# Windowed attention and a SoLU layer on one core: the second and fourth tile's first product in two other PSUM banks, the opening's list laid out anew, the last eviction by ScalarE alone

## The chip, the cores and the metric

The kernel runs on one core of a Trainium2 chip. The metric is the device time of one execution in microseconds. The engines are TensorE (PE; its weight loads are shown as PEld), VectorE (DVE), ScalarE (ACT), GpSimd (POOL) and SyncE (SP, which here only issues DMAs). Each engine works through its own instructions in order and waits on semaphores for the others. PSUM, into which TensorE writes, has eight banks of 512 float32 per partition.

## The reference

Two parts, one after the other. First, attention with a causal window over 8 batches, 8 heads, 576 positions and 64 channels per head; heads 0 to 3 look back over 32 neighbouring positions, heads 4 to 7 over 32 positions that lie 4 apart:

```python
scores = scale * np.matmul(q, k.transpose(0, 1, 3, 2))
rel = pos[:, None] - pos[None, :]
mask_plain = (rel >= 0) & (rel < window)                                  # window = 32
mask_dil = (rel >= 0) & (rel < window * dilation) & (rel % dilation == 0) # dilation = 4
scores = np.where(masks[None, :, :, :], scores, -1000000000.0)
scores = scores - np.max(scores, axis=-1, keepdims=True)
attn = np.exp(scores)
attn = attn / (np.sum(attn, axis=-1, keepdims=True) + 1e-09)
return np.matmul(attn, v)
```

Its result, 4608 tokens of 512 values (8 heads of 64), is the input x of the second part:

```python
h = x @ w_in                                   # 512 -> 1024
e = np.exp(h - h_max)
sm = e / (np.sum(e, axis=-1, keepdims=True) + 1e-09)
solu = h * sm
mu = np.mean(solu, axis=-1, keepdims=True)
var = np.mean((solu - mu) ** 2, axis=-1, keepdims=True)
ln = (solu - mu) / np.sqrt(var + 1e-06) * g_ln
return (ln @ w_out)                            # 1024 -> 512
```

The weights w_in and w_out arrive as 64-bit floats, and the kernel turns them into 32-bit ones on the chip.

## The kernel before, in words

**Attention in units.** A unit is a pair of heads of one batch; there are 32 (`n` = 0 to 31), four to a batch, of which the first two are plain and the last two dilated. For each unit the steps are: `S` (scores, TensorE, lines 175 to 198, into banks 2 and 3), `mask` (DVE), `max` (DVE), `sub` (subtract the maximum), `exp` (ACT), `sum` and `inv` (DVE), `norm` (multiply by the inverse sum), `turn` (32x32 transposes, DVE), `V` (the product with v, TensorE, line 265, into banks 4 to 7), `xh` (ACT, the rounded high part of the result, line 283) and `xl` (DVE, what the rounding left over, line 286). For units 0 to 3 TensorE itself adds the mask (line 183), so `mask` is empty and `sub` runs on DVE; for the others `mask` is a DVE instruction and `sub` runs on Pool. `norm` runs on DVE, unless a unit is in `POOL_NORM`, which is empty.

**The second part in tiles.** A tile is 128 tokens; there are 36 (`i` = 0 to 35). The first product (lines 293 to 305) has 24 matmuls, in four groups of six: `ha`, `hb` make the left half of the 1024 columns (bank 0), `hc`, `hd` the right half (bank 1). `ha` and `hc` read the part of x that comes from units 0 and 1 of the batch, `hb` and `hd` that from units 2 and 3. Each product is made of three, high by high, high by low and low by high, so that the result is nearly that of full float32. Then `peak` (DVE, the row maximum, line 310), `e` (ACT, exponential, line 317), `gate` (DVE, the product of both, line 324, which is the last to read banks 0 and 1), `mid` (centring, on ACT for tiles 0 to 3, otherwise on DVE), `var` (ACT, with six small instructions on Pool), `t` (eight transposes on TensorE into banks 3 and 4, line 357), `th` (ACT) and `tl` (DVE), which copy the high and the low part of the transposed tile, `o` (the second product, 24 matmuls, line 387, bank 2) and `out` (ACT scales, SP stores). `ps_h` is one pair of banks, 0 and 1, for all tiles, so the first product of a tile can begin only when the gate of the tile before has been read.

**The weights.** Each of 16 blocks (`b`; 0 to 7 of w_in, of which b//2 is the group of 128 input channels and b%2 the column half; 8 to 15 of w_out) is loaded (`w`, 512 KB) and converted: `low` and `abs` (ACT), `sign`, `clamp`, `join` (DVE), for w_out also `gain` (ACT), then `hi` (ACT, the rounded high part) and the low part. The latter goes one of two ways, by `LOW_DIFF`: for "m" TensorE makes the difference in PSUM with an identity (`diff`, lines 475 and 476, bank 5 + b % 3) and ACT copies it (`lo`, line 482); for "p" Pool subtracts (`lo`, line 484). So `hd0`, the last group of the first tile's first product, needs blocks 0 to 7 and units 0 to 3. The words of block b lie in a buffer that is shared: blocks 6 to 11 take those of blocks 0 to 5, blocks 12 and 13 those of 8 and 9, blocks 14 and 15 those of 10 and 11, and a load waits until its buffer has been read.

**The order.** It is written out by hand: `INIT` (first loads) and `OPENING` (everything up to the second product of tile 4) are lists of words, a step and its number, and the instructions of each engine are issued in the order of these words (lines 517 to 519). A word such as `S4` is one unit's scores; `q8`, `v8`, `w6` are loads, all of which stand in SP's one queue; a load of q, k or v takes the buffer of the unit four before and waits until that has been read. From tile 6 on (`FIRST`) the fixed list `STEP` is gone through once for each tile; tile 35 and what follows have `LAST` and `END`. When the opening's list ends, units 0 to 9 have been through `turn`, units 0 to 8 through `xl`, the second product has been made for tiles 0 to 4, and tile 5 has been transposed. The next words are `ha6` and the rest of the step for tile 6.

**The end.** The last tile's result lies in bank 5 and is evicted by `moe_out_last` in two halves, one by ACT and one by DVE, and stored in two halves, one on ACT's queue and one on SP's.

Of the kernel before, what the change touches and what calls it, by code (L numbers as in the profile page):

```python
# [14 lines left out]
AF = mybir.ActivationFunctionType  # L15
ALU = mybir.AluOpType
# [10 lines left out]
NTILE = NTOK // P  # L27
# [10 lines left out]
PE_MASK = (0, 1, 2, 3)  # L38
POOL_SUB = True
POOL_NORM = ()  # L40
# [42 lines left out]
def windowed_attention_then_solu_kernel(  # L83
# [13 lines left out]
    nc = tc.nc  # L97
# [16 lines left out]
    mask_sb = const.tile([P, 2, NS * WQ], BF16, name="mask_sb")  # L114
# [9 lines left out]
    ps_h = banks[:, 0:2, :]  # L124
# [471 lines left out]
```

## Time and profile before

| | us |
|---|---|
| median of three runs | 567.88 (567.01 to 571.52) |
| the profiled execution | 567.52 |
| its span, from the first to the last instruction | 565.7 |
| TensorE busy, share of the span | 531.3, 94% |
| VectorE busy | 358.2, 63% |
| ScalarE busy | 237.3, 42% |
| GpSimd busy | 110.6, 20% |
| mean granted TensorE clock | 0.982 |

A row of a group names line, engine, operation, output <- inputs by the program's names, shapes and count, then the busy time, the mean of one in ns, the idle time of the engine ahead of it and what ended most of that. A row of the timeline gives start and length in us, and in brackets the idle time of the engine before it and its releaser. A row of the chain gives start, length and the work. A row of the waits says which instruction waited for which: us in total, times, the longest. A row of the windows gives the busy time of each engine in a stretch of the span, then the granted clock, the share of the DMA engines and GB/s. Durations include some overlap: the next instruction of an engine starts before the one before has ended by the profile.

### The profile page before, as it was taken

How to read it: one execution, taken by the hardware profiler on the slowest of the kernel's cores; microseconds unless marked ns; L12 is line 12 of the kernel's file. 1: busy time of each engine (PE TensorE's matmuls, PEld its weight loads, DVE VectorE, ACT ScalarE, POOL GpSimd, SP SyncE). 2: the span in 40 equal slices, each digit the busy share in tenths (PEclk: the TensorE clock that was granted, in tenths of full speed). 3: DMA queues.
4: the chain of work that ended last, by engine and by line, in shares of the span. 5: the costliest groups of instructions: out<-in, count | busy, mean ns of one | idle time of the engine just before them, and what ended most of it. 6: DMA issues, size and time to landing. Idle time of an engine off the chain costs nothing.

```text
span 565.7 us, 16593 instructions
## 1 busy us (share of the span) xinstructions
PE 531.3 (94%) x7424; PEld 422.9 (75%) x7424; DVE 358.2 (63%) x555; ACT 237.3 (42%) x386; POOL 110.6 (20%) x256
## 2 busy tenths in 40 slices
PE   2775799899999999999999999999999999999997
PEld 1443588678888888888888888888888888888885
DVE  2989865576667766567667766567667766533342
ACT  3679754334344333433344333433344333433232
POOL 0002451123112222112112222112112222111111
PEclk9799889899999999999999999999999999999999
DMA  8976102332322233112222222123321000001001
GB/s 304 399 287 237 57 1 93 110 103 93 93 93 92 93 93 93 48 64 93 92 93 93 93 92 93 48 65 93 93 93 48 21 21 21 20 19 38 19 20 37
DMA packets 22103, 51.66 MB, mean 91 GB/s; under 512 B 2704, under 2 KB 3216, under 8 KB 22032
## 3 DMA queue, kind: packets, MB, share of 16 engines
q1 hardware_dynamic: 21888, 50.48, 26.4%
q8 instruction: 58, 0.95, 0.7%
q10 hardware_dynamic: 144, 0.13, 0.1%
q14 instruction: 13, 0.11, 0.1%
HBM read 41.16 MB, written 9.44 MB: 89 GB/s over the span
## 4 chain that ended last, share of the span: by engine, by line
PE 88%; DVE 5%; ACT 3%; issue 2%; DMA 1%; SPq 1%; ACTq 0%
PE banks L299 36%; PE banks L387 36%; PE banks L357 5%; PE banks L265 5%; PE banks L191 5%; DMA id_sb<-ident 1%; DVE x_lo L286 1%; DVE low L450 1%; DVE mag L458 1%; ACT x_hi L283 1%; PE banks L475 1%; DVE mag L443 1%; ACT low L437 0%; ACT w_i L482 0%; DVE nmax L310 0%
## 5 line engine op out<-in xcount | busy, mean ns | idle before, releaser
L299 PE MATMUL banks<-w_i,x_hi 128*128 128x512 f32 x576 | 188.9, 409 | 8.3 <-DVE mu L324 7.7
L387 PE MATMUL banks<-w_o,th 128*128 128x512 f32 x576 | 183.0, 401 | 0.0
L299 PEld LDWEIGHTS banks<-w_i,x_hi 128*128 128x128 f32 x576 | 105.1, 192 | 31.6 <-DVE mu L324 8.1
L387 PEld LDWEIGHTS banks<-w_o,th 128*128 128x128 f32 x576 | 107.0, 189 | 23.9
L299 PE MATMUL banks<-w_i,x_lo 128*128 128x512 f32 x288 | 115.0, 399 | 0.6 <-DVE x_lo L286 0.5
L387 PE MATMUL banks<-w_o,tl 128*128 128x512 f32 x288 | 112.8, 395 | 0.0
L310 DVE TENSOR_REDUCE nmax<-banks 128x1 f32<-128x1024 f32 x36 | 44.1, 1224 | 66.9 <-PE banks L299 66.9
L230 ACT ACTIVATE sm<-sm 128x640 f32<-128x640 f32 x32 | 23.5, 737 | 132.0 <-POOL sm L226 128.6
L317 ACT ACTIVATE e<-banks,nmax 128x1024 f32<-128x1024 f32 x36 | 40.2, 1117 | 65.9 <-DVE nmax L310 62.9
L372 DVE TENSOR_TENSOR tl<-banks,th 128x512 fp32r<-128x512 f32 x72 | 46.4, 685 | 32.3 <-ACT th L364 32.3
L299 PEld LDWEIGHTS banks<-w_i,x_lo 128*128 128x128 f32 x288 | 55.1, 191 | 14.3 <-DVE x_lo L286 1.4
L226 POOL TENSOR_TENSOR sm<-sm,mx 128x640 f32<-128x640 f32 x28 | 35.4, 1263 | 151.0 <-DVE mx L217 150.9
L387 PEld LDWEIGHTS banks<-w_o,tl 128*128 128x128 f32 x288 | 54.5, 189 | 12.8
L341 ACT ACTIVATE e<-t 128x1024 f32<-128x1024 f32 x36 | 38.2, 1061 | 49.6 <-DVE t L336 49.5
L205 DVE TENSOR_TENSOR sm<-banks,mask_sb 128x640 f32<-128x640 f32 x28 | 23.1, 824 | 54.5 <-PE banks L191 54.4
L364 ACT CAST th<-banks 128x512 fp32r<-128x512 f32 x72 | 38.8, 590 | 36.8 <-PE banks L357 36.7
L324 DVE CUSTOM_DVE_ANT_0 t<-banks,e 128x1024 f32<-128x1024 f32 x36 | 44.0, 1223 | 15.1 <-ACT e L317 12.0
L265 PEld LDWEIGHTS banks<-pt,vt 32*64 32x64 f32 x2816 | 33.8, 130 | 16.8 <-issue 9.0
L265 PE MATMUL banks<-pt,vt 32*64 32x64 f32 (+3 forms) x2816 | 37.3, 227 | 4.7 <-DVE pt L249 3.6
L191 PEld LDWEIGHTS banks<-kt,qt 64*32 64x32 f32 x2560 | 29.0, 109 | 15.0 <-issue 14.2
L357 PE MATMUL banks<-id_sb,t 128*128 128x128 f32 x288 | 37.5, 273 | 0.5 <-DVE x_lo L286 0.5
L357 PEld LDWEIGHTS banks<-id_sb,t 128*128 128x128 f32 x288 | 33.6, 141 | 5.8 <-DVE x_lo L286 0.8
(54 smaller groups left out, 469.5 us busy)
## 6 DMA issues: line engine op xcount, KB each, us to landing
vt<-vw SPq DMA_DIRECT2D x32, 384.0 KB, 3.6
kt<-kT SPq DMA_DIRECT2D x32, 312.0 KB, 3.1
qt<-qT SPq DMA_DIRECT2D x32, 296.0 KB, 4.1
out<-ob SPq DMA_DIRECT2D x35, 256.0 KB, 2.0
t<-w_in SPq DMA_DIRECT2D x6, 512.0 KB, 6.8
t<-w_out SPq DMA_DIRECT2D x4, 512.0 KB, 6.8
raw<-w_out SPq DMA_DIRECT2D x4, 512.0 KB, 4.7
raw<-w_in SPq DMA_DIRECT2D x2, 512.0 KB, 8.4
```

Source lines behind the costliest of these rows:

```text
L191: nc.tensor.matmul(out=ps_s[WIN * c : WIN * c + WIN, h, WQ * i : WQ * i + WQ], lhsT=qt[D * h : D * h + D, q0 : q0 + WIN], rhs=kt[D * h : D ...
L226: eng.tensor_tensor(out=st[n]["sm"], in0=st[n]["sm"], in1=wide(mx), op=ALU.subtract)
L265: nc.tensor.matmul(out=ps_x[D * h : D * h + D, c, c0 : c0 + k1 - k0], lhsT=vt[WIN * c : WIN * c + WIN, i, D * h : D * h + D], rhs=pt[WIN * ...
L299: nc.tensor.matmul(out=ps_h[:, half, :], lhsT=a[:, kt, xs], rhs=w_i[:, kt, half, part, :], start=(kt == 0 and k == 0), stop=(kt == KT - 1 ...
L310: nc.vector.tensor_reduce(out=nmax, in_=h, axis=AX.X, op=ALU.max, negate=True)
L317: nc.scalar.activation(out=e, in_=h, func=AF.Exp, bias=nmax, scale=1.0, accum_out=se)
L324: nc.vector.tensor_tensor_reduce(out=t, in0=h, in1=ms[i]["e"], scale=1.0, scalar=0.0, op0=ALU.mult, op1=ALU.add, accum_out=mu,)
L341: nc.scalar.activation(out=e, in_=t, func=AF.Square, accum_out=sq)
L357: nc.tensor.transpose(out=ps[:, f, :], in_=ms[i]["t"][:, k * P : k * P + P], identity=id_sb)
L364: nc.scalar.copy(out=th[:, 4 * c : 4 * c + 4], in_=ps_t[c].rearrange("p (f q) -> p f q", q=P))
L372: nc.vector.tensor_tensor(out=tl[:, fs], in0=ps_t[c].rearrange("p (f q) -> p f q", q=P), in1=ms[i]["th"][:, fs].bitcast(F32), op=ALU.subtract,
L387: nc.tensor.matmul(out=ps_o if i < NTILE - 1 else ps_last, lhsT=a[:, f, :], rhs=w_o[:, f, part, :], start=k == 0, stop=k == 3 * FT - 1,)
```

## The change

Five things are altered, the first four of them in the opening.

1. `ps_h` becomes a list: the first product of tiles 1 and 3 goes to banks 6 and 7 instead of 0 and 1; `peak`, `e` and `gate` read it there. `V` still writes banks 4 to 7.
2. `INIT` loads w0 first, the mask in two halves (`m0`, `m1`), and the gains later. `OPENING` has a new order; it contains the same words without `diff6` and `diff7`.
3. `LOW_DIFF`: the low parts of blocks 6 and 7 are made by Pool instead of by TensorE and ACT.
4. `POOL_NORM`: the `norm` of units 0, 2 and 4 to 9 runs on Pool instead of DVE.
5. `moe_out_last`: one ACT instruction evicts the whole of the last tile; the two stores stay where they are.

Of the new order, this much on each engine, as far as the prediction speaks of it. TensorE: `S0 S1 diff1 diff0 diff2 diff3 V1 S2 V0 S3 hc0 diff4 diff5 V2 V3 ha0 hb0 S5 ha1 hd0 S4 hb1 hc1 S7 ha2 hd1 hb2 hc2 hd2 V5 V4 ha3 S6 hc3 t0 hb3 hd3 ha4 t1 o0 V6 o1 V7 hc4 S9 t2 hd4 hb4 t3 o2 ...`; before it was `... hc0 diff4 V2 S3 ha0 diff6 diff7 diff5 V3 hd0 hb0 S5 hc1 ha1 S4 hd1 hb1 t0 hc2 hd2 ha2 hb2 t1 o0 hc3 S7 V4 ...`.

```diff
--- before.py
+++ after.py
@@ -36,43 +36,44 @@
 NEG = -1e30
 SIGN_BIT = -(1 << 31)
 PE_MASK = (0, 1, 2, 3)
+ALT = (1, 3)
 POOL_SUB = True
-POOL_NORM = ()
+POOL_NORM = (0, 2, 5, 4, 6, 7, 9, 8)
 ACT_CENTRE = (0, 1, 2, 3)
 Q_BUFS, V_BUFS, T_BUFS, TH_BUFS, CONV_BUFS = 4, 4, 4, 2, 4
 REBIAS = 2.0**16
 F64_MIN = REBIAS * float(np.array(0x38000000, np.uint32).view(np.float32))
 F64_MAX = REBIAS * float(np.array(0x47EFFFFF, np.uint32).view(np.float32))
-LOW_DIFF = 'mmmmmmmmpppppppp'
+LOW_DIFF = 'mmmmmmpppppppppp'
 FIRST = 6
-INIT = "q0 ib m w0 w1 v0 i g q1 w2 w3 v1 q2 w4 w5 v2 q3 v3"
+INIT = "w0 q0 ib m0 i w1 v0 q1 w2 w3 v1 m1 q2 w4 w5 v2 g q3 v3"
 OPENING = (
-    "neg0 S0 q4 max0 low0 abs0 sign0 clamp0 low1 sub0 abs1 join0 w6 exp0 "
-    "sign1 hi0 sum0 clamp1 inv0 S1 q5 join1 w7 norm0 hi1 diff0 max1 low2 "
-    "abs2 turn0 lo0 sign2 low3 V0 v4 clamp2 abs3 sign3 xh0 join2 w8 clamp3 "
-    "hi2 sub1 join3 w9 exp1 S2 q6 xl0 hi3 sum1 diff1 low4 max2 abs4 "
-    "diff2 inv1 lo1 sign4 low5 norm1 diff3 lo2 clamp4 abs5 turn1 lo3 join4 w10 "
-    "V1 v5 sub2 hi4 sign5 exp2 clamp5 xh1 sum2 low6 xl1 abs6 inv2 hc0 "
-    "low7 sign6 abs7 norm2 diff4 clamp6 turn2 lo4 join6 low8 V2 v6 sign7 hi6 "
-    "clamp7 S3 q7 abs8 join5 w11 xh2 join7 sign8 ha0 hi7 max3 hi5 xl2 "
-    "sub3 diff6 clamp8 exp3 join8 w12 diff7 lo6 sum3 gain8 diff5 inv3 lo7 norm3 "
-    "low10 lo5 turn3 low11 sign10 V3 v7 low9 sign11 abs10 sign9 xh3 clamp10 abs11 "
-    "xl3 abs9 clamp11 hd0 join10 w14 hi8 clamp9 gain10 lo8 hb0 hi10 join11 w15 "
-    "low12 lo10 peak0 gain11 abs12 S5 q9 join9 w13 e0 sign12 clamp12 gain9 gate0 "
-    "hi11 hi9 join12 hc1 lo11 low14 mask5 mid0 ha1 sign14 low15 lo9 max5 S4 "
-    "q8 var0 sign15 hd1 low13 sub5 mask4 abs14 hb1 abs15 sign13 abs13 t0 peak1 "
-    "gain12 th0 clamp14 clamp15 e1 clamp13 join14 join15 gain14 gate1 gain15 hi12 join13 hc2 "
-    "hi14 lo12 tl0 mid1 hd2 lo14 max4 gain13 ha2 hi15 sub4 hi13 var1 hb2 "
-    "lo15 exp4 t1 peak2 lo13 exp5 th1 sum4 o0 sum5 e2 inv4 tl1 norm4 "
-    "gate2 turn4 hc3 out0 inv5 mid2 norm5 S7 q11 var2 turn5 V4 v8 mask7 "
-    "ha3 xh4 max7 xl4 hd3 sub7 t2 exp7 o1 th2 sum7 inv7 tl2 norm7 "
-    "V5 v9 out1 S6 q10 turn7 xh5 xl5 hb3 mask6 max6 o2 peak3 sub6 "
-    "e3 exp6 gate3 sum6 V7 v11 out2 inv6 mid3 norm6 hc4 turn6 xh7 S8 "
-    "q12 var3 xl7 V6 v10 mask8 max8 ha4 xh6 sub8 xl6 t3 hd4 th3 "
-    "exp8 hb4 tl3 sum8 o3 peak4 inv8 e4 norm8 turn8 gate4 out3 mid4 hc5 "
-    "var4 t4 ha5 th4 hd5 tl4 hb5 S9 q13 peak5 V8 v12 mask9 e5 "
-    "max9 o4 xh8 gate5 sub9 xl8 exp9 mid5 sum9 var5 inv9 norm9 t5 out4 "
-    "turn9 th5 tl5 "
+    "low0 abs0 sign0 clamp0 join0 w6 S0 q4 hi0 neg0 max0 low1 sub0 abs1 "
+    "sign1 exp0 clamp1 sum0 S1 q5 join1 w7 inv0 hi1 max1 norm0 low2 diff1 "
+    "sub1 abs2 low3 diff0 sign2 abs3 clamp2 sign3 exp1 join2 w8 lo1 clamp3 hi2 "
+    "sum1 lo0 diff2 join3 w9 low4 inv1 hi3 turn0 abs4 diff3 norm1 low5 sign4 "
+    "abs5 turn1 lo3 lo2 clamp4 sign5 V1 v5 join4 w10 low6 S2 q6 clamp5 "
+    "xh1 join5 w11 sign6 hi4 xl1 hi5 abs6 max2 V0 v4 low7 clamp6 abs7 "
+    "sub2 xh0 join6 S3 q7 exp2 xl0 hi6 sum2 hc0 lo6 max3 inv2 low10 "
+    "sub3 norm2 abs10 diff4 exp3 sign7 diff5 lo4 turn2 low8 sum3 lo5 clamp7 abs8 "
+    "inv3 V2 v6 join7 low9 norm3 hi7 xh2 sign10 lo7 turn3 abs9 xl2 low11 "
+    "sign8 V3 v7 abs11 sign9 ha0 sign11 xh3 clamp10 xl3 clamp8 clamp9 hb0 clamp11 "
+    "join10 w14 join8 w12 S5 q9 gain10 join9 w13 gain8 ha1 mask5 gain9 join11 "
+    "w15 hi10 hd0 max5 hi8 lo10 gain11 S4 q8 peak0 hi9 sub5 hb1 hi11 "
+    "mask4 e0 max4 lo8 hc1 exp5 gate0 sub4 S7 q11 low14 sum5 low12 ha2 "
+    "lo9 abs14 inv5 exp4 hd1 mid0 sign14 norm5 sum4 hb2 low13 peak1 var0 lo11 "
+    "hc2 turn5 abs12 inv4 hd2 e1 sign12 sign13 low15 norm4 gate1 abs13 abs15 sign15 "
+    "V5 v9 turn4 xh5 clamp14 clamp12 mid1 xl5 var1 clamp13 V4 v8 clamp15 join14 "
+    "xh4 join12 gain14 xl4 gain12 join13 ha3 hi14 join15 gain13 lo14 mask7 gain15 peak2 "
+    "hi12 S6 q10 hi13 lo12 max7 hi15 hc3 mask6 e2 lo13 max6 t0 gate2 "
+    "hb3 lo15 th0 hd3 tl0 sub6 mid2 ha4 var2 peak3 sub7 exp6 t1 e3 "
+    "sum6 o0 inv6 th1 gate3 norm6 exp7 tl1 turn6 sum7 V6 v10 out0 inv7 "
+    "mid3 norm7 o1 xh6 turn7 var3 xl6 V7 v11 out1 hc4 xh7 xl7 S9 "
+    "q13 mask9 max9 t2 hd4 sub9 th2 hb4 tl2 exp9 sum9 t3 peak4 o2 "
+    "th3 inv9 e4 tl3 norm9 gate4 turn9 mid4 ha5 out2 var4 S8 q12 hc5 "
+    "mask8 max8 hd5 sub8 hb5 exp8 t4 peak5 o3 th4 sum8 e5 inv8 tl4 "
+    "norm8 gate5 turn8 mid5 V8 v12 out3 var5 o4 xh8 xl8 t5 out4 th5 "
+    "tl5 "
 )
 STEP = "ha.i hb.i S.n q.n mask.n max.n sub.n hc.i hd.i V.m v.m peak.i exp.n sum.n inv.n e.i gate.i mid.i xh.m xl.m var.i norm.n turn.n o.j t.i th.i tl.i out.j"
 LAST = "ha.i hb.i hc.i hd.i peak.i e.i gate.i mid.i oa.j t.i oz.j th.i tl.i out.j var.i"
@@ -121,7 +122,7 @@
     x_hi = const.tile([P, KT, RING], F32R, name="x_hi")
     x_lo = const.tile([P, KT, RING], F32R, name="x_lo")
     banks = psum.tile([P, 8, 512], F32, name="banks")
-    ps_h = banks[:, 0:2, :]
+    ps_h = [banks[:, 6:8, :] if i in ALT else banks[:, 0:2, :] for i in range(NTILE)]
     ps_o = banks[:, 2, :]
     ps_last = banks[:, 5, :]
     ps_s = banks[:, 2:4, 0 : NS * WQ]
@@ -297,7 +298,7 @@
             xs = slice(c0, c0 + P)
             for k, (a, part) in enumerate(((x_hi, 0), (x_hi, 1), (x_lo, 0))):
                 nc.tensor.matmul(
-                    out=ps_h[:, half, :],
+                    out=ps_h[i][:, half, :],
                     lhsT=a[:, kt, xs],
                     rhs=w_i[:, kt, half, part, :],
                     start=(kt == 0 and k == 0),
@@ -305,12 +306,12 @@
                 )
 
     def moe_peak(i):
-        h = ps_h.rearrange("p a b -> p (a b)")
+        h = ps_h[i].rearrange("p a b -> p (a b)")
         nmax = ms[i]["nmax"] = small.tile([P, 1], F32, name="nmax")
         nc.vector.tensor_reduce(out=nmax, in_=h, axis=AX.X, op=ALU.max, negate=True)
 
     def moe_exp(i):
-        h = ps_h.rearrange("p a b -> p (a b)")
+        h = ps_h[i].rearrange("p a b -> p (a b)")
         nmax = ms[i]["nmax"]
         e = moe.tile([P, DF], F32, name="e", bufs=1)
         se = small.tile([P, 1], F32, name="se")
@@ -318,7 +319,7 @@
         ms[i]["e"], ms[i]["se"] = e, se
 
     def moe_gate(i):
-        h = ps_h.rearrange("p a b -> p (a b)")
+        h = ps_h[i].rearrange("p a b -> p (a b)")
         t = ms[i]["t"] = moe.tile([P, DF], F32, name=f"t{i % T_BUFS}", bufs=1)
         mu = ms[i]["mu"] = small.tile([P, 1], F32, name="mu")
         nc.vector.tensor_tensor_reduce(
@@ -403,13 +404,9 @@
         m = DO // 2
         rows = slice(i * P, i * P + P)
         ob = moe.tile([P, DO], F32, name="ob", bufs=1)
-        left, right = ob[:, :m], ob[:, m:]
-        nc.scalar.activation(out=left, in_=ps_last[:, :m], func=AF.Copy, scale=ms[i]["rstd"])
-        nc.vector.tensor_scalar(
-            out=right, in0=ps_last[:, m:], scalar1=ms[i]["rstd"], scalar2=None, op0=ALU.mult
-        )
-        nc.scalar.dma_start(out=out[rows, :m], in_=left)
-        nc.sync.dma_start(out=out[rows, m:], in_=right)
+        nc.scalar.activation(out=ob, in_=ps_last, func=AF.Copy, scale=ms[i]["rstd"])
+        nc.scalar.dma_start(out=out[rows, :m], in_=ob[:, :m])
+        nc.sync.dma_start(out=out[rows, m:], in_=ob[:, m:])
         del ms[i]
 
     cv = {}
@@ -496,7 +493,7 @@
         "i": lambda _: nc.sync.dma_start(out=id_sb, in_=ident),
         "ib": lambda _: nc.sync.dma_start(out=id_bf, in_=ident_bf),
         "g": lambda _: nc.sync.dma_start(out=g_sb, in_=g_ln),
-        "m": lambda _: nc.sync.dma_start(out=mask_sb, in_=mask),
+        "m": lambda d: nc.sync.dma_start(out=mask_sb[:, d], in_=mask[:, d]),
         "neg": lambda _: nc.scalar.mul(out=minus, in_=id_sb, mul=-1.0),
         "abs": conv_abs, "low": conv_low, "clamp": conv_clamp, "sign": conv_sign,
         "join": conv_join, "gain": conv_gain, "hi": conv_hi, "diff": conv_diff, "lo": conv_lo,
```

## The prediction

> **What bounds the kernel now.** I read the page first, then the busy time by stage, the waits and the chain of waits of the stage that shows idle time. Page, part 1:
>
> ```profile
> PE 531.3 (94%) x7424; PEld 422.9 (75%) x7424; DVE 358.2 (63%) x555; ACT 237.3 (42%) x386; POOL 110.6 (20%) x256
> ```
>
> The share of 94% is an average over two regimes. The stages are cut at the end of the first tile's first product (51.24) and at the start of tile 6's (142.03), which is where both opening lists end:
>
> ```profile
> 0.00:51.24 51.24, 31.47 (x736) 19.04 (x743) 38.16 (x68) 33.00 (x54) 1.76 (x5) 0.93 0.86 313
> 51.24:142.03 90.79, 79.88 (x1218) 64.46 (x1218) 62.23 (x98) 47.25 (x76) 28.74 (x50) 0.92 0.27 85
> 142.03:554.64 412.61, 412.61 (x5447) 333.58 (x5445) 256.01 (x387) 153.77 (x252) 79.08 (x199) 1.00 0.20 66
> ```
>
> Columns are window, length, busy PE, PEld, DVE, ACT, POOL, granted clock, DMA share, GB/s. From 142.03 on TensorE has no idle time and full clock; the change leaves that order as it is, so nothing is to be had or lost there. The first window is bound by the weights' conversion on DVE and ACT and by DMA (share 0.86). The second holds 90.79 - 79.88 = 10.9 us of idle TensorE at a clock of 0.92. Its waits, and the chain:
>
> ```profile
> PE banks L299 <- DVE mu L324: 7.7, 2, 3.9
> PE banks L191 <- issue: 2.0, 1, 2.0
> PE banks L265 <- DVE x_lo L286: 0.6, 1, 0.6
> PE banks L357 <- DVE x_lo L286: 0.5, 1, 0.5
> ```
>
> ```profile
> 56.15 5.30 PE banks L299 x12
> ...
> 62.41 2.97 PE banks L299 x12
> ...
> 70.03 7.36 PE banks L299 x24
> ...
> 83.84 1.39 PE banks L299 x6
> 85.23 0.97 PE banks L191 x64
> ...
> 91.44 5.58 PE banks L387 x24
> ...
> 101.27 2.17 PE banks L299 x6
> 103.44 2.56 PE banks L387 x7
> ...
> 508.38 5.51 PE banks L299 x24
> ```
>
> The two waits on L324 are tile 1's and tile 2's first product waiting until the gate has read banks 0 and 1. After each the same matmuls run slowly: 12 in 5.30 instead of 2.97, 24 in 7.36 instead of 5.51, and after the "issue" gap 6 in 2.17 instead of 1.39 and 7 in 2.56 instead of 7/24 of 5.58. That is 2.33 + 1.85 + 0.78 + 0.93 = 5.9 us lost to clock. So this stage loses 10.9 + 5.9 = 16.8 us, the sum that can be won back after the first product.
>
> **The change, term 1: the time to the first product (hd0).** Now ACT's first instruction waits for the identity, and the conversion behind it:
>
> ```profile
> ACT minus L500 <- DMA id_sb<-ident: 8.4, 1, 8.4
> ```
>
> With w0 first in SP's list and neg0 behind hi0, ACT begins when the first 512 KB have landed, about 4.4 by the rate below, instead of 10.4. DVE has 59 instructions up to xl3 (two for each inv) at 38.16/68 = 0.56 each, 33 us; if it never waited, xl3 would end near 38. It will wait, because ACT is in order and low10 now stands ahead of exp3 and xh2. Block 10's bytes are late:
>
> ```profile
> vt<-vw SPq DMA_DIRECT2D x32, 384.0 KB, 3.6
> kt<-kT SPq DMA_DIRECT2D x32, 312.0 KB, 3.1
> qt<-qT SPq DMA_DIRECT2D x32, 296.0 KB, 4.1
> ...
> t<-w_in SPq DMA_DIRECT2D x6, 512.0 KB, 6.8
> ```
>
> ```profile
> 0.00:32.00 32.00, 17.44 (x455) 10.63 (x455) 20.31 (x38) 17.80 (x30) 0.19 (x4) 0.89 0.97 357
> ```
>
> Up to w10 the new SP list moves 11 blocks of 512 KB, 6 pairs of q and k (608), 5 of v (384) and 260 KB of mask, identities and gains: 11,460 KB, 11.7 MB. The DMA engines are full (0.97) and have moved 357 x 32 = 11.4 MB by 32.0; so w10 is there at about 33.5 (0.7 of it an allowance for reporting). Then come nine ACT instructions (low10 to hi7) at 33.00/54 = 0.61, to 39.0; xh2 and xl2; V3, xh3, xl3. One such unit, read from the chain:
>
> ```profile
> 114.20 1.09 PE banks L265 x70
> ...
> 115.32 1.22 ACT x_hi L283
> ...
> 116.57 1.22 DVE x_lo L286
> ```
>
> xh2 and xl2 take 2.4, to 41.4; the unit from V3 to xl3 takes 117.8 - 114.2 = 3.6, to 45.0. DVE is no later: sum3 to turn3 are eight instructions after exp3 (35.3), 4.5 us, to 39.8. Then hb0, S5, ha1, hd0: 3 x 1.39 + 0.97 = 5.1, to 50.1. That is 1.1 before the 51.24 of now, and S5 and ha1 (2.4 us), which now come later, are done by then: 3.5 us won. Ends: 38 + 5.1 = 43 if DMA holds nothing up, 10 won; or nothing won, if the two pieces put ahead only shift hd0 back. I take 3.5, since the byte row is the one that binds. The two differences taken from TensorE (diff6, diff7) and two ACT copies lie where TensorE is idle anyway and count nothing; if TensorE were the bound there, about 2 x 1.1 us would be won.
>
> **Term 2: the losses after it.** From a product's end to its gate's end took 4.9 us both times (51.24 to 56.15; 3.9 of it shows as the wait, since S stands under the rest). New order: after hd0 stand S4, hb1, hc1, S7, 2 x 0.97 + 2 x 1.39 = 4.7, so ha2 waits 0.2 to 0.4 for gate0. That is what banks 6 and 7 buy: 7.7 us of waits and their slow clock go. What is late next is the price of the same banks: V5 must wait for gate1 (hd1's end + 4.9, against hb2, hc2, hd2 = 4.2: 0.8 us). And V4 waits for xl5 as ha3 waits for xl4, because V writes banks 4 to 7 and nothing stands between on TensorE. A plain unit's two copies:
>
> ```profile
> 87.66 0.64 ACT L283 CAST x_hi<-banks 128x576 fp32r<-128x576 f32 x1 [0.75 <-PE banks L265]
> ...
> 88.33 0.76 DVE L286 TENSOR_TENSOR x_lo<-banks,x_hi 128x576 fp32r<-128x576 f32 x1 [0.26 <-ACT x_hi L283]
> L205 DVE TENSOR_TENSOR sm<-banks,mask_sb 128x640 f32<-128x640 f32 x28 | 23.1, 824 | 54.5 <-PE banks L191 54.4
> ```
>
> 0.64 + 0.76 = 1.4 for each, 0.3 more where a clamp stands ahead of xl5: 3.1 us. S6 waits for mask7, which stands behind join13 and join15 on DVE (0.6), t0 for mask6 (0.3), and t2, right behind S9 in banks 3 and 4, for mask9 (0.8 by the 824 ns row). Together 0.4 + 0.8 + 3.1 + 0.6 + 0.3 + 0.8 = 6.0. Behind gaps of this size the clock may fall:
>
> ```profile
> 102.00:104.00 2.00, 2.00 (x6) 1.61 (x5) 1.51 (x3) 0.00 (x0) 0.90 (x1) 0.51 0.84 270
> ```
>
> This is the clock after the single 2.0 us "issue" gap; it cost 0.78 + 0.93 = 1.7, and I charge that once for the V5, V4, ha3 gaps, which lie within 5 us. I also keep 2.0 for an instruction stall, as now, since the number of TensorE instructions hardly changes. Total 6.0 + 1.7 + 2.0 = 9.7, and 16.8 - 9.7 = 7.1 won. Ends: 2.8 lost (the two bank waits alone, 14.0 won) and 16.8 lost (nothing won); below nothing is the slower rival's case.
>
> The Trainium skill, "TensorE: Matmul & The Clock Gate", section "Why this matters for your kernels", says that the clock falls back only for idle gaps of about 3 us. By it my charge of 1.7 would go and the sum be 1.7 us better; the row above, half clock behind a 2.0 us gap, speaks for keeping it.
>
> **Term 3: Pool.** Ten full-size instructions come to Pool: lo6, lo7 and eight norms. Off DVE go eight norms. Where they meet, a row pair shows the price:
>
> ```profile
> 49.66 1.74 POOL L484 TENSOR_TENSOR w_o<-mag,w_o 128x512 fp32r<-128x512 f32 x1 [49.24 <-ACT w_o L469]
> 50.14 1.55 DVE L443 TENSOR_SCALAR mag<-mag 128x512 f32<-128x512 f32 x1
> L443 DVE TENSOR_SCALAR mag<-mag 128x512 f32<-128x512 f32 x16 | 7.7, 493 | 0.0
> L244 DVE TENSOR_TENSOR sm<-sm,rs 128x640 f32<-128x640 f32 x32 | 26.2, 819 | 0.1
> ```
>
> The clamp took 1.55, its mean is 0.49: about 1.1 us lost to one Pool instruction. Before hd0 four such stand (norm0, lo6, norm2, lo7), and two norms (1.6) leave DVE: between -1.6 and 4.5 - 1.6 = +2.9 us. I take 0: DVE then has slack, because it waits on block 10's bytes anyway.
>
> **Term 4: the end.** The last eviction is now two halves, one after the other:
>
> ```profile
> 562.17 0.47 ACT L407 ACTIVATE ob<-banks,rstd 128x256 f32<-128x256 f32 x1 [3.86 <-PE banks L387]
> ...
> 562.68 0.48 DVE L408 TENSOR_SCALAR ob<-banks,rstd 128x256 f32<-128x256 f32 x1 [5.45 <-ACT ob L407]
> L397 ACT ACTIVATE ob<-banks,rstd 128x512 f32<-128x512 f32 x35 | 24.5, 701 | 16.7 <-PE banks L387 13.3 <-issue 3.4
> ```
>
> One instruction of 0.70 from 562.17 ends at 562.87 instead of 563.16: 0.3 won for SP's store, at most; ACT's own starts 0.2 later and both now leave together. I take 0.2.
>
> **Sum.** 3.5 + 7.1 + 0 + 0.2 = 10.8. The profiled execution took 567.5 (span 565.7 and 1.8 around it), so 556.7; the median of the runs shown is 0.4 above it, which I leave in the range.
>
> **The rivals.** (a) The replanned opening runs dense: the first stage wins 5, only the two bank waits are left: 567.5 - 5 - 14.0 - 0.2 = 548.3. For it: most gaps above are under 1 us and sit in places where one list step decides. Against: both copies of V5 and V4 lie bare.
> (b) Pool takes the time back. The four Pool instructions ahead of hd0 each stop a DVE instruction (2.9 net), and norm5 and norm4 behind it twice more (2.3): 5.2 worse, 561.9. For it: the row pair; against: 28 units' subtractions (4 to 31) have run on Pool all along while DVE's norm stayed at 819 ns on average. The Trainium skill, "SBUF — State Buffer", section "Who interferes with whom", makes it a rule: Vector and GpSimd instructions that want the shared ports exclude each other for a whole instruction. The row pair agrees.
> (c) The opening is not earlier (term 1 is 0): 560.2. A late w7 or a half clock in ha0 and hb0 would do it.
> (d) Slower: w15. In SP's list w13 and w15 stand behind q9, which waits for S5, and S5 now stands behind hb0. low15, abs13 and abs15 stand on ACT right ahead of xh5, so V4, ha3 and all behind them wait for w15's landing one for one. I expect its issue at about 48.5 and landing at 53 to 57 (rows: 6.8 us for a block), while ACT reaches low15 near 60. It costs from 60 on, and makes the kernel 1% slower only when it lands at 60 + 10.8 + 5.7 = 76 or later, say 574. Nothing in the trace shows a block taking 20 us.
> (e) The new waits eat the whole gain: 564 to 568.
>
> **How the numbers follow.** What a measurement here can tell from no change is about 1%, 5.7 us, so faster means under 562.2. Forecast 0.45, (a) 0.15, (b) 0.20, (c) 0.10, (d) 0.05, (e) 0.05. Faster: 0.45 + 0.15 + 0.10 and a little over half of (b), 0.81; within 1%: 0.14; slower: 0.05. The range leaves out about half of (a), (d) and (e): 549.0 to 563.5.
>
> **What would show it.** In the changed profile the waits of L299 on L324 should be gone or under 1 us, with waits on x_lo L286 of 1 to 2 us twice in their place around 63 to 68; ACT's first low near 4.4 and low10 near 33.5; hd0's end near 50; tile 6's first product at 131 and the rest after it 412.6 long with clock 1.00. It would be wrong if hd0 ends past 54, if DVE rows of over 1.5 us pile up beside Pool's, or if low15 waits for DMA.

## The result and the profile after

The changed kernel took 561.97 us (median of 4 runs, 561.24 to 562.76), the kernel before, run on the same chip, 568.62 (567.01 to 571.52). The ratio is 0.988 with an interval of 0.985 to 0.991: 1.2% faster, 6.7 us, where 10.8 were forecast. Every ratio below is likewise to the kernel before, run beside it on the same chip; its median moves between 567.57 and 568.62 from one set to the next, so the ratios are compared rather than the microseconds. Two executions ran in a slower state and are left out of the medians and intervals: one of the kernel before at 601.26 us, beside the first four experiments, and one of the kernel with `ha0` ahead at 1009.02. The profiled execution of the changed kernel took 562.46 us with a span of 560.7, against 565.7 before: 5.0 us between the two traces. Lines after 38 of the program have moved by one or more; L300 is now the first product, L266 is `V`, L192 and L184 are `S`, L388 is the second product.

Page of the changed kernel, part 1:

```profile
PE 530.6 (95%) x7418; PEld 423.8 (76%) x7418; DVE 353.0 (63%) x546; ACT 235.8 (42%) x384; POOL 121.3 (22%) x266
```

Busy time says nothing here: TensorE does the same work in both, but for the four matmuls of `diff6` and `diff7`. The stages, cut at the same places as before (end of the first tile's first product, start of tile 6), with columns window, length, PE, PEld, DVE, ACT, POOL, granted clock, DMA share, GB/s:

```profile
0.00:55.65 55.65, 35.99 (x816) 24.01 (x823) 40.24 (x70) 33.47 (x54) 6.56 (x9) 0.82 0.80 295
55.65:136.91 81.26, 74.74 (x1131) 60.40 (x1132) 55.36 (x88) 45.11 (x74) 34.66 (x55) 0.94 0.29 91
136.91:549.63 412.72, 412.72 (x5447) 333.74 (x5447) 256.10 (x387) 153.79 (x252) 79.10 (x199) 1.00 0.21 66
```

The first stage became 4.41 us longer (51.24 to 55.65), the second 9.53 shorter (90.79 to 81.26), the rest is unchanged (412.61 and 412.72, clock 1.00). The forecast was 50.1 and 131 for the two cuts. (In the new order `hd0` is the last group of that product; in the kernel before it was `hb0`, whose end is the 51.24.) `S5` and `ha1`, 2.36 us of work at full clock ("warm" below), moved from the second stage into the first, so the real balance is 2.05 lost before `hd0`'s end and 7.17 won after it.

TensorE's waits over the whole span (total, times, longest); "issue" is time in which the engine waited for nothing that the profile shows:

```profile
...
PE banks L266 <- DVE x_lo L287: 4.8, 2, 3.2
PE banks L192 <- issue: 4.1, 2, 3.2
PE banks L266 <- DVE mu L325: 2.5, 1, 2.5
...
PE banks L300 <- DVE x_lo L287: 1.5, 1, 1.5
...
PE banks L358 <- DVE sm L206: 0.9, 1, 0.9
```

The two waits of the first product on the gate (7.7 us before) are gone. One wait on a gate (L325) is there, but it is `V`'s (L266), as the new banks demand. Of the 4.8 us on `x_lo` at L266, 3.16 are `V3`'s in the first stage and 1.60 are `V4`'s. The other new lines are where the forecast put them, except the 4.1 us of "issue". The chain of waits of the changed kernel (start, length, work) shows that "issue" stands in the first stage:

```profile
26.44 3.19 issue
...
33.33 0.90 issue
...
35.34 2.70 PE banks L300 x6
...
42.63 1.10 ACT x_hi L284
...
45.02 1.48 PE banks L266 x62
46.50 5.23 PE banks L300 x12
...
52.70 2.95 PE banks L300 x12
...
76.45 2.93 PE banks L300 x6
```

A 3.19 us gap six matmuls before the end of `S2`, another of 0.90 in `S3`, then `hc0` at half clock (2.70 for six, 1.39 warm), the difference of block 4, ACT's copy of it at 39.17, `xh2`, `xl2`, and `V3` at 45.02. `ha0` and `hb0` take 5.23 instead of 2.97. ACT's list shows what TensorE's lateness did to the way from `low10` to `V3`:

```profile
34.60 0.76 ACT L434 ACTIVATE low<-raw,below 128x512 int32<-128x512 uint16 x1 [1.09 <-DMA raw<-w_out]
...
37.25 0.74 ACT L231 ACTIVATE sm<-sm 128x640 f32<-128x640 f32 x1 [1.33 <-DVE sm L224]
39.17 0.59 ACT L479 CAST w_i<-banks 128x512 fp32r<-128x512 f32 x1 [1.18 <-PE banks L473]
```

These are `low10`, `exp3` and `lo4`: ACT waits 1.33 us for what `S3` leads to and 1.18 for `diff4`.

### The profile page after: what moved, and what is told of

Read it like the earlier page. It is cut to its first block, busy times and chain, and to the rows that moved or that the text cites. A ratio compares the mean times of both kernels' runs of the same rounds, so it can differ in the third digit from the quotient of the medians.

```text
span 560.7 us, 16574 instructions
## 1 busy us (share of the span) xinstructions
PE 530.6 (95%) x7418; PEld 423.8 (76%) x7418; DVE 353.0 (63%) x546; ACT 235.8 (42%) x384; POOL 121.3 (22%) x266
## 4 chain that ended last, share of the span: by engine, by line
PE 91%; DMA 3%; DVE 2%; ACT 2%; issue 1%; ACTq 0%
PE banks L300 37%; PE banks L388 37%; PE banks L266 6%; PE banks L358 6%; PE banks L192 6%; DMA raw<-w_in 2%; DMA kt<-kT 1%; DMA t<-w_in 1%; ACT low L434 0%; DVE x_lo L287 0%; DVE low L447 0%; ACT w_i L479 0%; ACT x_hi L284 0%; ACT mag L424 0%; DVE pt L250 0%
## 5 line engine op out<-in xcount | busy, mean ns | idle before, releaser
L300 PE MATMUL banks<-w_i,x_hi 128*128 128x512 f32 x576 | 189.4, 410 | 1.5 <-DVE x_lo L287 1.5
L388 PE MATMUL banks<-w_o,th 128*128 128x512 f32 x576 | 182.4, 400 | 0.0
L300 PEld LDWEIGHTS banks<-w_i,x_hi 128*128 128x128 f32 x576 | 105.8, 193 | 24.6 <-DVE x_lo L287 1.6
L388 PEld LDWEIGHTS banks<-w_o,th 128*128 128x128 f32 x576 | 106.3, 188 | 23.5
L300 PE MATMUL banks<-w_i,x_lo 128*128 128x512 f32 x288 | 114.9, 399 | 0.0
L388 PE MATMUL banks<-w_o,tl 128*128 128x512 f32 x288 | 112.5, 395 | 0.0
L300 PEld LDWEIGHTS banks<-w_i,x_lo 128*128 128x128 f32 x288 | 55.3, 192 | 13.0
L388 PEld LDWEIGHTS banks<-w_o,tl 128*128 128x128 f32 x288 | 54.2, 188 | 12.7
L325 DVE CUSTOM_DVE_ANT_0 t<-banks,e 128x1024 f32<-128x1024 f32 x36 | 44.0, 1222 | 13.8 <-ACT e L318 10.8
L266 PEld LDWEIGHTS banks<-pt,vt 32*64 32x64 f32 x2816 | 35.3, 138 | 20.6 <-issue 8.6
L266 PE MATMUL banks<-pt,vt 32*64 32x64 f32 (+3 forms) x2816 | 38.9, 235 | 9.3 <-DVE x_lo L287 4.8
L192 PEld LDWEIGHTS banks<-kt,qt 64*32 64x32 f32 x2560 | 29.7, 112 | 16.9 <-issue 16.5
L192 PE MATMUL banks<-kt,qt 64*32 64x64 f32 x2560 | 35.8, 238 | 4.1 <-issue 4.1
```

The costliest lines, as they stand in the source:

```text
L192: nc.tensor.matmul(out=ps_s[WIN * c : WIN * c + WIN, h, WQ * i : WQ * i + WQ], lhsT=qt[D * h : D * h + D, q0 : q0 + WIN], rhs=kt[D * h : D ...
L266: nc.tensor.matmul(out=ps_x[D * h : D * h + D, c, c0 : c0 + k1 - k0], lhsT=vt[WIN * c : WIN * c + WIN, i, D * h : D * h + D], rhs=pt[WIN * ...
L300: nc.tensor.matmul(out=ps_h[i][:, half, :], lhsT=a[:, kt, xs], rhs=w_i[:, kt, half, part, :], start=(kt == 0 and k == 0), stop=(kt == KT - ...
L325: nc.vector.tensor_tensor_reduce(out=t, in0=h, in1=ms[i]["e"], scale=1.0, scalar=0.0, op0=ALU.mult, op1=ALU.add, accum_out=mu,)
L388: nc.tensor.matmul(out=ps_o if i < NTILE - 1 else ps_last, lhsT=a[:, f, :], rhs=w_o[:, f, part, :], start=k == 0, stop=k == 3 * FT - 1,)
```

## The experiments

**The banks alone.** Does the gain come from the banks, or from the order? The kernel before with only tile 1 in banks 6 and 7, all lists untouched (the old order would overwrite tile 3's banks before they are read, so tile 3 stays):

```diff
+ALT = (1,)
...
-    ps_h = banks[:, 0:2, :]
+    ps_h = [banks[:, 6:8, :] if i in ALT else banks[:, 0:2, :] for i in range(NTILE)]
...
```

> The kernel before with only the second tile's first product in banks 6 and 7 (nothing else of the change). Theory A, the banks are where the gain is: tile 1's and tile 2's waits for the gate (3.9 and 3.8) and their half clock (4.2) go, the first product ends at 51.2 as before, and 5 to 10 us are won, 558.5 to 563.5. Theory B, the weights' conversion is next in line: its last low part lands at 79.5 as before, the second product of tile 0 cannot run ahead of it and waits at its eighth block, and only about 3 us are won, 565.

It took 564.28 us (6 runs, 560.91 to 565.59), ratio 0.993 (0.990 to 0.996). Its waits of TensorE:

```profile
PE banks L192 <- DVE mu L333: 3.3, 1, 3.3
PE banks L192 <- issue: 3.2, 2, 2.0
PE banks L388 <- POOL w_o L485: 1.6, 1, 1.6
```

The gate's waits have gone, and others took part of their place: a 3.3 us wait of the next scores behind DVE, and the weights' conversion (Pool's last low parts hold the second product for 1.6). By the medians about 3.3 us of the gain are the banks' (of tile 1 alone), and the other 3.4 need the new order. The two intervals touch between 0.990 and 0.991, so the split is rough. The new order without the banks was not run: it puts `ha1` ahead of `hd0`, into a bank that still holds tile 0's left half.

**The norms.** Rival (b) had Pool take the gain back. The changed kernel with all norms on DVE again:

```diff
-POOL_NORM = (0, 2, 5, 4, 6, 7, 9, 8)
+POOL_NORM = ()
```

> The changed kernel with all norms back on VectorE. Theory A, Pool's full-size instructions hold up VectorE ahead of the second tile's gate: the two signs that took 2.30 take 1.2, the wait of V5 for that gate (2.5) loses about 1, but two norms of 0.75 now stand there: within 0.7 us of the changed kernel, 561.3 to 562.7. Theory B, taking norms off VectorE is a gain in itself: 2 us slower, 564.

561.65 us (561.47 to 561.83), ratio 0.990 (0.989 to 0.992): no difference. The collisions are real, though. In the changed kernel's timeline, ahead of the gate that `V5` waits for:

```profile
65.51 1.30 POOL L481 TENSOR_TENSOR w_o<-mag,w_o 128x512 fp32r<-128x512 f32 x1
65.62 1.22 DVE L239 TENSOR_SCALAR rs<-rs 128x10 f32<-128x10 f32 x1
...
67.01 2.30 DVE L447 SCALAR_TENSOR_TENSOR low<-t,low 128x512 int32<-128x512 int32 x2
67.17 1.59 POOL L245 TENSOR_TENSOR sm<-sm,rs 128x640 f32<-128x640 f32 x1 [0.36 <-DVE rs L240]
```

and in the same place with the norms on DVE:

```profile
65.36 1.30 POOL L481 TENSOR_TENSOR w_o<-mag,w_o 128x512 fp32r<-128x512 f32 x1
65.37 0.13 DVE L239 TENSOR_SCALAR rs<-rs 128x10 f32<-128x10 f32 x1
65.67 2.15 DVE L447 SCALAR_TENSOR_TENSOR low<-t,low 128x512 int32<-128x512 int32 x2
67.74 0.81 DVE L245 TENSOR_TENSOR sm<-sm,rs 128x640 f32<-128x640 f32 x1
```

A 128x10 instruction, 0.13 in the second kernel, takes 1.22 in the first, where it starts 0.11 after Pool's low part and ends with it. In the second kernel the same low part is there, but the 128x10 instruction starts 0.01 after it and is not held; the two sign instructions behind it take 2.15 instead. So one of the two stops stays and moves to the next DVE instruction, the other (the signs beside Pool's norm) goes, and DVE has the norm itself (0.81) back.

**The table load.** ACT's first low part came at 6.58, not 4.4. The trace shows why; ACT in the changed kernel:

```profile
5.28 1.28 ACT L434 ACT_TABLE_LOAD   x1 [5.28 <-DMA t<-w_in]
6.58 0.75 ACT L434 ACTIVATE low<-t,below 128x512 int32<-128x512 uint16 x1
```

The table load (at 0.72 before, ahead of an instruction that then waited 8.40 us for the identity by itself) now stands behind the wait for w0: here the trace has a separate semaphore instruction of L434 on ACT's queue at 5.2, ahead of the load, and in the kernel before it has none. A one-column activation put first, whose operands need no DMA:

```diff
+    first = const.tile([P, 1], F32, name="first")
+    nc.scalar.activation(out=first, in_=mhalf, func=AF.Identity, bias=below, scale=1.0)
```

> The changed kernel with a one-column ScalarE instruction ahead of all others, so that the table load (1.28 us) runs before the first block lands. ScalarE's first conversion then starts at 5.3 instead of 6.6. Theory A, ScalarE's start sets the first stage: the first product ends 1.3 us earlier, 560.7. Theory B, the landing of later blocks and TensorE's instruction stalls set it: the first product moves by less than 0.4, 562.0.

The first low part came at 5.24, 1.3 earlier, `hd0` ended at 55.06, 0.6 earlier, and the time was 562.27 (561.82 to 563.47), ratio 0.992 (0.990 to 0.993): no difference. (In the traces with the norms on DVE and with the copies first, whose loads stand as in the changed kernel, `hd0` ends at 55.57 and 55.50, so 0.1 to 0.2 is the spread.) The missed term exists, but is not what holds the first stage.

**The issue gaps.** In the changed kernel the DMA engines run full while `S2` stands still. Two kernels tell the DMA's load from the place of the loads in the queue. The first holds six loads back until `V0`, so that the engines have little to do around 24 to 26, where `S2` begins:

```diff
-  S0 q4 hi0 ... S1 q5 join1 ... join2 w8 lo1 ... join3 w9 low4 ... S2 q6 clamp5 ... join5 w11 sign6 ... V0 v4 low7
+  S0 hi0 ... S1 join1 ... join2 lo1 ... join3 low4 ... S2 clamp5 ... join5 sign6 ... V0 v4 w8 w9 w11 q5 q4 q6 low7
```

> The changed kernel with the loads of q4, q5, q6, w8, w9 and w11 placed behind v4 (which waits for V0), so that the DMA engines run dry between about 26 and 31 us. Theory A, TensorE's issue gaps of 3.2 and 0.9 us in S2 and S3 come from the full DMA engines, through which its instructions arrive too: both together fall under 1.5, blocks 7 and 10 land 3 us earlier, the first product ends near 51 instead of 55.7, and the time is 557 to 559. Theory B, the gaps belong to the place in the instruction stream: they stay near 3 and the first product moves by 1 at most, 561.

The second only moves q4 and q5 behind w10, so that w10 comes earlier and the engines stay full:

```diff
-  S0 q4 hi0 ... S1 q5 join1 ... join4 w10 low6
+  S0 hi0 ... S1 join1 ... join4 w10 q4 q5 low6
```

> The changed kernel with the loads of q4 and q5 behind that of w10, nothing held back: blocks 7 and 10 land up to 3 us earlier, and the DMA engines stay full between 24 and 31 us. This tells the two readings of the run with loads held back apart. Theory A, the instruction gaps under full DMA engines set the first stage: the gaps stay at 3 to 4 us in total, the first product ends within 1 us of 55.7, time 561 to 562.5. Theory B, the landing of blocks 7 and 10 sets it: the first product ends near 53, 559.

With the loads held: 559.06 us (557.49 to 560.16), ratio 0.985 (0.983 to 0.988), `hd0`'s end at 52.49, 3.2 earlier (the stage shows the gain clearly; the interval of the ratio still overlaps the changed kernel's). With q4 and q5 behind: 561.79 (560.84 to 562.33), ratio 0.989 (0.985 to 0.993), `hd0`'s end at 54.87. TensorE's wait and the window from 24 to 26 (the last column is GB/s; it is 400 in the changed kernel), loads held:

```profile
PE banks L191 <- issue: 1.4, 1, 1.4
```

```profile
24.00:26.00 2.00, 2.00 (x108) 1.45 (x95) 0.89 (x2) 0.69 (x2) 0.00 (x0) 0.58 0.47 133
```

and with q4 and q5 behind:

```profile
PE banks L191 <- issue: 5.2, 2, 3.7
```

```profile
24.00:26.00 2.00, 1.80 (x103) 1.27 (x93) 0.65 (x1) 0.66 (x1) 0.00 (x0) 0.76 1.04 414
```

With q4 and q5 behind, `low10` starts at 33.30 and no longer waits for its block, yet the gaps are as long and `V3` is no earlier (45.67). So it is the load on the DMA engines, not the landing of block 10. The other traces agree: the gap in `S2` is 2.68 to 3.72 us in the six kernels that have the new order with the engines full, and 0.89 to 1.54 in the four that hold the loads back. The DMA queues show the way: TensorE's program comes over the same engines, 0.95 MB in 58 packets, 16 KB each. (The page does not name the queue's engine; of 16,574 instructions 14,836 are TensorE's, and this queue moves 0.95 of the 1.06 MB of instructions.) In the changed kernel, TensorE's timeline and then the queue in the window from 27.0 to 27.2 (queue, packets, MB, share):

```profile
23.31 1.20 PE L266 MATMUL banks<-pt,vt 32*64 32x32 f32 x84 [0.16 <-ACT w_i L479]
...
25.09 1.35 PE L192 MATMUL banks<-kt,qt 64*32 64x64 f32 x74
29.63 0.43 PE L192 MATMUL banks<-kt,qt 64*32 64x64 f32 x6 [3.19 <-issue]
```

```profile
q8 instruction: 58, 0.95, 0.7%
```

```profile
q8 instruction: 1, 0.02, 34.2%
```

(The line with 58 packets is from part 3 of its page, the last one from that window.) With the loads held the same pieces stand like this, and the packet moves in the window from 25.0 to 25.2:

```profile
23.23 1.09 PE L265 MATMUL banks<-pt,vt 32*64 32x32 f32 x84 [0.16 <-ACT w_i L478]
...
24.86 1.35 PE L191 MATMUL banks<-kt,qt 64*32 64x64 f32 x74
27.62 0.43 PE L191 MATMUL banks<-kt,qt 64*32 64x64 f32 x6 [1.41 <-issue]
```

```profile
q8 instruction: 1, 0.02, 34.0%
```

TensorE stops at the same matmul, the 75th of `S2`, and goes on about 2.6 us after the packet in both (29.63 and 27.62). With q4 and q5 behind, the packet moves at 26.8 and TensorE goes on at 29.53; in the kernel before, it is 35.8 and 38.44 (the end of `S3`). What differs is when the packet moves: 3.7 us after `V1`'s last piece began where the engines are full, 1.8 where they are not. The load is not all of it. In the kernel before, the gap of 1.32 us in `S3` came when the engines moved 144 GB/s (35 to 36), and the gap of 1.97 at 98.97, whose packet moves at 98.2, when they moved 5 GB/s (96 to 99). So a gap of 1 to 2 us is there without the load, and the load adds about 2. That a gap needs a dense run of small matmuls is argued, not tested: `V1`, `S2`, `V0` and `S3` are 352 of them almost in one piece in the new order, while in the kernel before the differences of the blocks, a few long matmuls each, stood between them as long as the engines were full.

The Trainium skill, "Runtime: NRT & Kernel Launch", section "Instruction fetch mechanics", says that the program is fetched in 16 KiB blocks while the current one is executed, and that crossing a block is mostly hidden. The packets agree with the block; the gaps of 3.19 and 3.7 us show a place where it is not hidden.

**`ha0` ahead of `V3`.** `ha0` and `hb0` run at half clock behind the 3.16 us wait of `V3`, in which the granted clock fell (1.00 from 43 to 44, 0.78 from 44 to 45, 0.50 from 45 to 51). `ha0` needs only units 0 and 1 of x, so it can fill that wait:

```diff
-  V2 v6 join7 ... V3 v7 abs11 sign9 ha0 sign11
+  V2 v6 ha0 join7 ... V3 v7 abs11 sign9 sign11
```

> The changed kernel with ha0 ahead of V3 on TensorE, into the 3.2 us that TensorE waits there for x_lo. Theory A, ha0 and hb0 at half clock behind that gap (5.23 us against 2.97) are what delays hd0 past xl3: the first product ends 2 to 3 us earlier, 559 to 560. Theory B, hb0 waits for xl3 (49.0) anyway: the first product ends 0.5 to 1 earlier, 561.3.

561.66 us (three runs, 560.99 to 563.14), ratio 0.989 (0.983 to 0.996). `hd0` ended at 54.47, 1.2 earlier, although the issue gaps ahead of it were 4.4 us (2.68 + 1.75) instead of 4.1 and `V3` began 1.4 later (46.43). The half clock is gone (granted clock 1.00 from `V3` to `hd0`): this stretch takes 8.0 us, where it took 10.6 with `ha0` (1.39 at full clock) in it. `xh3` and `xl3` now hold TensorE in it for 0.39 and 0.50, so the later `V3` and these waits take back part of what the clock gives. The time does not tell it from the changed kernel: inconclusive alone.

**Copies first.** After `hd0` the idle time is `V5`'s, `V4`'s and `ha3`'s, 2.47 + 1.60 + 1.52. Here DVE gets the gate, the transposition and the two `xl` ahead of the signs (but for `sign12`) and clamps of blocks 12 to 15, ACT gets `e` and `th` ahead of the gains, and Pool's low part of block 11 goes ahead of its norm:

```diff
-  lo9 abs14 ... e1 sign12 sign13 low15 norm4 gate1 abs13 abs15 sign15 V5 v9 turn4 xh5 clamp14 clamp12 mid1 xl5 var1 clamp13 V4 ...
+  lo9 lo11 abs14 ... e1 norm4 gate1 sign12 low15 V5 v9 turn4 abs13 abs15 xh5 xl5 mid1 var1 V4 v8 sign13 sign15 clamp14 xh4 xl4 ha3 ...
```

> The changed kernel with VectorE's list turned around behind the second tile's first product: gate1, turn4, xl5 and xl4 ahead of the conversion's signs, clamps and joins, lo11 ahead of norm5 on Pool, e and th ahead of the gains on ScalarE. Theory A, V5, V4 and ha3 are late by what stands ahead of them on VectorE: their waits (2.5, 1.6, 1.5) fall to under 0.5, 1.4, 1.4, the half clock behind them goes, 4 to 6 us are won, 556 to 558. Theory B, the conversion of blocks 12 to 15 then ends later and the first second product waits for Pool's last low part: 1 to 2 us won, 560.5.

561.32 us (561.11 to 562.06), ratio 0.988 (0.984 to 0.992): no difference, less than either theory gave. TensorE's timeline and the chain of this kernel:

```profile
70.18 1.53 PE L265 MATMUL banks<-pt,vt 32*64 32x32 f32 x96 [1.54 <-DVE mu L332]
73.93 1.22 PE L299 MATMUL banks<-w_i,x_hi 128*128 128x512 f32 x2 [2.22 <-DVE x_lo L286]
92.42 1.08 PE L265 MATMUL banks<-pt,vt 32*64 32x64 f32 x80 [1.42 <-DVE pt L249]
```

```profile
93.50 7.33 PE banks L387 x24
```

`V5` no longer waits, `ha3` starts 2.5 us earlier (76.45 to 73.93), and `V6` gives it back: it waits 1.42 for its normalised rows, and the second product behind it takes 7.33 instead of 5.78. Tile 6 starts at 136.49, where it started at 136.91. The chain ahead of `V6` (77.99 to 92.37) holds 9.5 us of DVE's work and 3.8 of ACT's; the conversion's joins, gain and `hi` are 2.6 of both. So what is late is DVE's list as a whole with ACT's behind it, and turning it round only shows the lateness elsewhere.

**All of it together.** Loads held, `ha0` ahead, copies first, table early, and the end of the kernel before (two halves); then the same without copies first, and the first again with the norms on DVE.

```diff
+    first = const.tile([P, 1], F32, name="first")
+    nc.scalar.activation(out=first, in_=mhalf, func=AF.Identity, bias=below, scale=1.0)
...
+  (the three list edits above)
...
-        nc.scalar.activation(out=ob, in_=ps_last, func=AF.Copy, scale=ms[i]["rstd"])
+  (moe_out_last as before)
```

> The changed kernel with the loads held back, ha0 ahead of V3, the copies first, ScalarE's table load early and the last eviction in two halves as before. If the parts add: 2.9 + 2.0 + 4.5 + 0.3 + 0.2 = 9.9 won on the changed kernel, 552. If the gain of an earlier first product is taken back by the conversion's end: 555.

> The kernel with all four parts, but VectorE's list behind the second tile's first product as the change has it. If turning the list around is worth what the run with it alone showed (0.6 us, the rest given back at V6), this takes 557.5 to 558; if it is worth more once the first product is early, 559.5.

> The kernel with all four parts and all norms back on VectorE. With gate1 and the copies first, norm4 and norm5 stand on VectorE between them, 0.75 each, and V6's turn6 no longer waits behind Pool's low parts. If Pool's queue sets V6 (it waits 1.4 for turn6), 555.5 to 556.5; if VectorE itself does, 557 to 558.5.

All together: 557.13 us (4 runs, 556.25 to 559.17), ratio 0.981 (0.977 to 0.986). Without copies first: 558.1 (5 runs, 555.65 to 559.01), 0.982 (0.979 to 0.984). With the norms on DVE: 558.5 (5 runs, 558.06 to 561.31), 0.985 (0.982 to 0.988). The stages of the first:

```profile
0.00:50.70 50.70, 34.27 (x816) 22.10 (x823) 39.01 (x70) 33.13 (x54) 5.61 (x9) 0.87 0.88 322
50.70:133.07 82.37, 74.82 (x1131) 60.06 (x1132) 53.87 (x88) 46.14 (x75) 36.43 (x56) 0.96 0.29 91
```

`hd0` ends at 50.7, where 50.1 was forecast for the changed kernel, and the second stage is no shorter than in that kernel (82.37 and 81.26). So the parts do not add up to the 552 of the expectation. The first two versions are 1.8 to 1.9% faster than the kernel before. Against the changed kernel's interval (0.985 to 0.991) the one without copies first is clear, the other two overlap it. The list turned round adds nothing that can be measured, and norms on Pool or on DVE are the same within the intervals.

## Why the prediction was right, and where it was not

The time of 561.97 lies in the range and on the forecast side, 1.2% faster, but 5 us above the number given. By its steps:

**Term 2, the losses after `hd0`, held.** Forecast: 9.7 us left of 16.8. Measured: the stage of 81.26 less its warm work, 90.79 - 16.8 - 2.36 = 71.63, is 9.63. The parts were less good than the sum, and that the sum comes out within 0.1 is luck: `V5` and the clock took 3.1 more than charged, the stall, `ha2`, `S6` and `t0` 3.3 less. Idle time is 81.26 - 74.74 = 6.5 against 6.0: `V4` and `ha3` 1.60 + 1.52 = 3.1 as forecast, `t2` 0.92 against 0.8, but `V5` 2.47 against 0.8, because the gate that it waits for was held by the two collisions shown above (about 1.1 for the 128x10 instruction, against the 0.13 of the other kernel, and 0.9 for the two signs, against twice 0.68), while `ha2`, `S6` and `t0` did not wait. (The prediction's 4.9 us from a product's end to its gate's end, "both times", was 4.9 and 4.65: the second is 65.38 to 70.03.) The clock took the other 3.1, not 1.7: `V4` and `ha3` are both slow (1.70 against 1.13, 2.93 against 1.39), then `S6` and `hc3`. And the 2.0 kept for an instruction stall did not come in this stage; it came in the first.

**Term 1, the time to the first product, is the step that failed.** It said 3.5 won, and 2.05 were lost: 5.55 off. It bound the stage by the bytes up to w10, and that reckoning was good (`low10` at 34.60 against 33.5, 1.1 late), but w10 was not the last to arrive. TensorE was: its gaps in `S2` and `S3`, and `hc0` at half clock behind them, put `sub3`, `exp3` and `diff4` back, and ACT stood still for 1.33 + 1.18 = 2.5 us on its way from `low10` to `xh2`. So `V3` began at 45.02 instead of 41.4, 3.6 late, and from there to `hd0` the clock of `ha0` and `hb0` cost 2.26 more (5.23 against 2.97), of which 0.3 was made up. The experiments give sizes of this order: holding the loads brings `hd0` 3.2 forward, `ha0` ahead 1.2, the table load 0.6. I had charged an issue stall once, after the first product, and had asked of the loads only when they land, not what else goes over their engines.

**Term 3, Pool, 0, held in total.** Norms on Pool or on DVE give the same time, so rival (b) falls, although its mechanism can be read in the trace. Its number, 561.9, is the nearest of all to the measured one, by coincidence: of the four Pool instructions that (b) names ahead of `hd0` (`norm0`, `lo6`, `norm2`, `lo7`) only `norm2` stops a DVE instruction (`sign7`, 1.36 instead of 0.68), and the loss that (b) charges to Pool is TensorE's in the trace. The Trainium skill's rule in "SBUF — State Buffer", section "Who interferes with whom", agrees with the rows (1.22 for an instruction that took 0.13 in the other run). In time the price was zero here, because without the norms on Pool the next DVE instruction met Pool's low part instead and DVE had the norm to do.

**Term 4, the end, did not win, and if anything had the wrong sign.** The last eviction and what follows it, from ACT's start to the end of the span, took 565.7 - 562.17 = 3.53 before. In the changed kernel:

```profile
556.99 0.69 ACT L407 ACTIVATE ob<-banks,rstd 128x512 f32<-128x512 f32 x1 [3.85 <-PE banks L388]
557.70 0.33 SPq L409 DMA_DIRECT2D out<-ob  x1
557.71 0.37 ACTq L408 DMA_DIRECT2D out<-ob  x1
```

```profile
out<-ob SPq DMA_DIRECT2D x1, 128.0 KB, 1.9
out<-ob ACTq DMA_DIRECT2D x1, 128.0 KB, 2.1
```

560.7 - 556.99 = 3.71, 0.2 more, where 0.2 less was forecast. The eviction is as quick as said, but both stores leave together and land in 2.1 and 1.9 us; before, half a microsecond apart, it was 1.8 and 1.7. In the other traces the old end took 3.56 to 3.64, the new one 3.65 to 3.73, so the loss is 0.1 on average, about the rounding of the span.

**The rivals.** (a), dense, did not come. (c), the opening not earlier, is the nearest in its mechanism: 560.2, and it named the half clock in `ha0` and `hb0`, though not its cause. (d) fell: `low15` follows its neighbour without idle time, so w15 was not late:

```profile
66.15 0.75 ACT L434 ACTIVATE low<-raw,below 128x512 int32<-128x512 uint16 x1
```

(e), the new waits eat the gain, fell with term 2.

**The clock.** The charge for half clock behind gaps of 1 to 2 us was right in kind and too small. The Trainium skill, "TensorE: Matmul & The Clock Gate", section "Why this matters for your kernels", names gaps of about 3 us. Here gaps of 2.47, 1.60 and 1.52 us within 9 us of time were followed by six matmuls in 2.93 instead of 1.39, so by that rule the charge would have gone and the sum would have been 1.7 us further off. Nor do gaps alone tell when the clock falls: in the changed kernel it fell to 0.50 at about 24.1, with no gap of TensorE above 1.03 us in the 13 us before, and came back at about 37.7. Whether the small matmuls that fill this time have a part in it was not tested.

**What stays open.** Which engine sets the stage after `hd0` as a whole: turning DVE's list round moved 2.5 us from `V5` to `V6` and no more. Why TensorE runs dry for 1 to 2 us at some packets, with the DMA engines nearly idle too, is not shown. Nor is it settled why the granted clock differs between runs of one kernel: the six runs of the banks alone go from 565.59 at a mean clock of 0.984 to 560.91 at 0.999.

## What to carry to other kernels

When a stage moves many bytes and TensorE works through many small matmuls in it, reckon TensorE's own program among the bytes: read the "issue" gaps beside the GB/s, and hold back the loads that nobody needs yet. A wait that is taken away by other buffers brings its gain only as far as the next engine is early; read what that engine does in the microseconds before, and forecast the sum of a stage rather than its single gaps. And an edit that costs nothing by its instructions (an eviction by one engine, a first instruction that now waits) still moves what hangs on it: here two stores and a table load.

## What the runs showed of the hardware

- TensorE's program arrives in 16 KB packets over the engines that the kernel's loads use; TensorE goes on about 2.6 us after such a packet moves, and with the engines at 400 GB/s the packet moved 3.7 us after a fixed point of the program, with the loads held (133 GB/s) 1.8 us after it. The gaps are 2.7 to 3.7 us in six kernels against 0.9 to 1.5 in four; one of 1.97 stood where the engines moved 5 GB/s.
- ACT's table load (1.28 us) can stand behind the wait of the first instruction: at 5.28, behind a semaphore instruction that waits for a DMA. It need not: in the kernel before it ran at 0.72, although its instruction then waited for a DMA until 10.40. Which of the two it is was not tested further; with a first instruction that needs no DMA it ran at 0.72.
- Two 128 KB stores that leave within 0.01 us land in 1.9 and 2.1 us; half a microsecond apart, in 1.7 and 1.8.
- A DVE instruction of 128x10 elements was stopped for 1.1 us by one of Pool's of 128x512 when it started 0.11 us after it, and took its 0.13 when it started 0.01 after it.
- The granted clock fell to 0.50 behind a single gap of 1.97 us, and at 24.1 in the changed kernel with no gap above 1.03 in the 13 us before.
